# Tile 0's output stores moved behind batch 2's values and into tile 2, a cast's buffer exchanged, and a split load cut elsewhere

## The chip, the cores and the metric

The kernel runs on one core of a Trainium2 chip. Its engines work side by side, each in its own program order: TensorE (PE, with a separate row PEld for weight loads), VectorE (DVE), ScalarE (ACT), GpSimd (POOL) and SyncE (SP). SP only issues transfers here; ACT and POOL issue some as well. The metric is the device time of one execution in microseconds (us). GB/s are those of the profile.

## The reference

Attention in a window of 32 positions to each side, for 8 batches of 8 heads, 576 positions and 64 features, and then a two-layer network with a tanh GELU on the 4608 tokens:

```python
scores = scale * np.matmul(q, k.transpose(0, 1, 3, 2))      # (8, 8, 576, 576)
mask = np.abs(pos[:, None] - pos[None, :]) <= 32
scores = np.where(mask, scores, -1000000000.0)
attn = softmax(scores)
x = np.matmul(attn, v).transpose(0, 2, 1, 3).reshape(4608, 512)
h = x @ w_in                                                # 512 to 2048
out = gelu_tanh(h) @ w_out                                  # 2048 to 512
```

Inputs and output are float32. The kernel computes in float16 with sums in float32.

## The kernel before, in words

**Tiles and batches.** The attention result of all tokens goes as `xT` (features on partitions) into a ring of 1536 tokens. The network runs over nine tiles of 512 tokens, `t` from 0 to 8; a batch has 576 tokens. While tile `t` is in work, the attention of batch `b = t + 1` is done in between. Each turn of the loop over `t` (L810) has two halves. In the first, `ffn_in` multiplies the tile by `w_in` in 16 columns (`fc`), each followed by a GELU on ACT (L540); for `t` from 1 on, DVE makes sums of the GELU's results (L575). In the second, `ffn_out` multiplies by `w_out`: tile 0 in the plain way (`ffn_out_0`), the later tiles with seven products of block sums (`WINO`), 112 steps `i`. The plans `PLAN_0`, `PLAN_1` and `PLAN` say at which step `i` a piece of attention is put between: `s` are the scores of a group of two heads (L427 on PE, the exponential on ACT, L439), `m` the mask on DVE (L445), `v` the sums and the product with V (L450, L460), `x` the result's way into `xT` (L495). PE does all of this in the order of the program, with no engine choosing for it.

**What a batch needs.** In the first half of a tile `cast_and_turn` casts the queries to float16 on DVE (L352), and SP sends them through a transposing transfer to `QT` (L355). `keys()` does the same for the keys (L375, and two transfers to `KT`, L377). The last 64 positions, the tail, go separately: `QT` once more and `KL`. The product with V wants V in two alignments; `pair_v` makes the second by copies on DVE (L192, L193). `load_qk` (L165) has SP load the queries, keys and tails of the batch after; from batch 3 on POOL loads V with a cast in the transfer (L183, L187), behind a small copy (L849) that waits until `KL` has landed.

**Batch 2 is special.** Its keys are cast at `fc == 3` of tile 1 (L822), its tail queries and tail keys on ACT (L361, L367) at `fc` 9 to 13. Its V comes in float32 by SP, in four chunks, issued at L383 behind the key transposes, into the buffer of an earlier query load, and its tail at L371. POOL casts the chunks (`cast_v`, L297, called at L830) and the tail (`cast_vt`, L294, called at step `i == 30` of tile 1, L912). DVE pairs four heads at `i == 17` and four at `i == 40` (L914).

**Tile 0's output.** `ffn_out_0` leaves four blocks of 128 tokens by 512, 256 KB each, in `later`, in the order of the blocks 0, 3, 1, 2 (L611). Entries 0 and 2 share a tile in the place `qt16` of the pool `hp`; entries 1 and 3 are in the pool `yp`. They are stored in tile 1: at `fc == 5` POOL issues 0 and 2 and ACT issues 1, at `fc == 6` ACT issues 3 (L825 to L828). All later tiles are stored by POOL, eight or nine transfers a tile (L594), with the last tile's by SP and ACT. The tail queries of each batch are cast into a tile of that place `qt16` too, and so wait until entries 0 and 2 are out.

**The beginning.** Batch 0's V chunks are loaded by SP at L151 and, the fourth, at L230, in two transfers of 120 and 8 partitions, followed in SP's order by `w_in` (L209). PE fills waits with `spin`, products that nobody reads. The first wait on V in batch 0 is behind POOL's casts (L297) and DVE's pairs (L198, L200); the fourth chunk is cast by DVE (L746) and ACT (L747).

Of the kernel before, what the change touches and what calls it, by code (L numbers as in the profile page):

```python
# [10 lines left out]
FP16 = mybir.dt.float16  # L11
# [25 lines left out]
def cut(b):  # L37
    return 120 if b else 128
# [33 lines left out]
def kernel(  # L72
# [9 lines left out]
    nc = tc.nc  # L82
# [3 lines left out]
    NPAIR = H // 2  # L86
# [15 lines left out]
    rawp = ctx.enter_context(tc.tile_pool(name="rawp", bufs=2))  # L102
    hp = ctx.enter_context(tc.tile_pool(name="hp", bufs=1))
# [85 lines left out]
    def pair_v(b, copy, hs=slice(0, H)):  # L189

        V = Vs[b % 2]
        copy(V[64:128, 4:8, hs, :], V[64:128, 0:4, hs, :])  # L192
        copy(V[0:64, 4:7, hs, :], V[0:64, 1:4, hs, :])  # L193
# [32 lines left out]
    qk(6)  # L226
    load_table(exp_set)
    vs(4, 0, 1, 2)
    for p in (slice(0, 120), slice(120, 128)):
        nc.sync.dma_start(raws[0][3][p, 3, :, :], v[0, :, 384 + p.start:384 + p.stop, :].rearrange("h p d -> p h d"))  # L230
    wi = []
    for i in range(4):
# [49 lines left out]
    def cast_open(b):  # L282
        halfs[b] = [hp.tile([128, NPAIR, 4, 2, 64], FP16, name="q16"),
                    hp.tile([128, NPAIR, 4, 2, 64], FP16, name="k16")]
        QTs[b] = ap_.tile([128, NPAIR, 4, 144], FP16, name="QT")
# [7 lines left out]
    def cast_vt(b):  # L293
        nc.gpsimd.tensor_copy(Vs[b % 2][0:64, 7, :, :], raws[b][4])  # L294

    def cast_v(b, c, copy=nc.gpsimd.tensor_copy):
        copy(Vs[b % 2][:, c, :, :], raws[b][3][:, c, :, :])  # L297
# [6 lines left out]
    def trans_tails(b, pt, half=slice(0, 128), copy=nc.vector.tensor_copy):  # L304
        t16 = halfs[b][2]
        for pr in range(NPAIR):
            nc.tensor.transpose(pt[:, pr, half], t16[half, 2 * pr:2 * pr + 2, :], idn[half, half])
        if half.stop > 64:
            copy(KLs[b % 2], pt[:, 0:4, 64:128])
        if half.start < 64:  # L310
            nc.vector.tensor_copy(QTs[b][:, :, :, 128:144],
                                  pt[:, 0:4, 0:64].rearrange("d r (p j) -> d r j p", j=4))
# [25 lines left out]
    def cast_and_turn(b):  # L338
        cast_open(b)
        q16, k16 = halfs[b]  # L340
        qr, kr, qt, kt = raws[b]
        small = {}

        def tails_of(which):
            if which not in small:
                small[which] = hp.tile([16, NPAIR, 4, 2, 64], FP16, name="qt16", tag="qt16") if which == "q" else \
                    hp.tile([64, NPAIR, 2, 64], FP16, name="kt16", tag="t16")
            return small[which]

        def queries(src, dst, p0, p1):  # L350
            for pr in range(NPAIR):
                nc.vector.tensor_copy(  # L352
                    dst[:, pr, :, :, :].rearrange("p j h d -> p h j d"),
                    src[:, 2 * pr:2 * pr + 2, :].rearrange("p h (j d) -> p h j d", j=4))
            nc.sync.dma_start_transpose(QTs[b].rearrange("d r j p -> d (r j) p")[:, :, p0:p1],  # L355
                                        dst.rearrange("p r j h d -> p (r j h d)"))

        def rest(i):
            qt16, kt16 = tails_of("q"), tails_of("k") if i == 4 else None
            if i < NPAIR:  # L360
                nc.scalar.copy(qt16[:, i, :, :, :].rearrange("p j h d -> p h j d"),  # L361
                               qt[:, 2 * i:2 * i + 2, :].rearrange("p h (j d) -> p h j d", j=4))
            if i == 3:
                nc.sync.dma_start_transpose(QTs[b].rearrange("d r j p -> d (r j) p")[:, :, 128:144],
                                            qt16.rearrange("p r j h d -> p (r j h d)"))
            if i == 4:
                nc.scalar.copy(kt16.rearrange("p r h d -> p (r h d)"), kt.rearrange("p h d -> p (h d)"))  # L367
                nc.sync.dma_start_transpose(
                    KLs[b % 2], kt16.rearrange("p r h d -> p (r h d)"))
                raws[b].append(tailp.tile([64, H, 64], FP32, name="vt", tag="vt"))  # L370
                nc.sync.dma_start(raws[b][4], v[b, :, 512:S, :].rearrange("h p d -> p h d"))  # L371

        def keys():
            for pr in range(NPAIR):
                nc.vector.tensor_copy(k16[:, pr, :, :, :], kr[:, :, 2 * pr:2 * pr + 2, :])  # L375
                if pr % 2:
                    nc.sync.dma_start_transpose(  # L377
                        KTs[b % 2][:, pr - 1:pr + 1, :].rearrange("d r (c p) -> d (r c) p", c=4),
                        k16[:, pr - 1:pr + 1, :, :, :].rearrange("p r c h d -> p (r c h d)"))
            if b == 2:  # L380
                vr = rawp.tile([128, 4, H, 64], FP32, name="qr")
                for c in range(4):
                    nc.sync.dma_start(vr[:, c, :, :],  # L383
                                      v[b, :, 128 * c:128 * c + 128, :].rearrange("h p d -> p h d"))
                raws[b] = [None, None, None, vr]

        queries(qr, q16, 0, 128)
        if b == 2:
            combine(2, nc.vector)
            combine(3, nc.vector)  # L390
            return keys, rest
        keys()
        qt16, kt16 = tails_of("q"), tails_of("k")
        queries(qt, qt16, 128, 144)
        nc.vector.tensor_copy(kt16.rearrange("p r h d -> p (r h d)"), kt.rearrange("p h d -> p (h d)"))
        nc.sync.dma_start_transpose(
            KLs[b % 2], kt16.rearrange("p r h d -> p (r h d)"))
# [140 lines left out]
    def gelu(t, n):  # L538
        fc = column(t, n)
        nc.scalar.activation(gTs[t][:, fc, :], phs[fc], AF.Gelu_apprx_tanh)  # L540
        if t and n % 4 == 3:
            sums(t, n // 4)
# [20 lines left out]
    def combine(i, eng):  # L563
        dst, x, y = wino["todo"][i]
        eng.tensor_tensor(dst, x, y, op=ALU.subtract)
# [14 lines left out]
    def store(t, t4, yo, cols=slice(0, 512), *engs):  # L580

        m = i = 0
        while m < 128:
            b, c = divmod(t * 512 + t4 * 128 + m, S)
            q0, n = (0, cut(b)) if c < 4 * cut(b) else (cut(b), 144 - cut(b))
            j, p = divmod(c - 4 * q0, n)
            e = min(n - p, 128 - m)
            nj = 1 if p else max(1, min(4 - j, (128 - m) // n))
            eng = engs[i % len(engs)] if engs else nc.gpsimd
            if nj > 1:  # L590
                e = nj * n
                eng.dma_start(out_v[b, j:j + nj, q0:q0 + n, cols], yo[m:m + e, cols])
            else:
                eng.dma_start(out_v[b, j, q0 + p:q0 + p + e, cols], yo[m:m + e, cols])  # L594
            m += e
            i += 1

    later = []
# [211 lines left out]
    for t in range(NT):  # L810
        b = t + 1
        att = b < B
        if t:
            for fc in range(begun):
                ffn_in(t, fc, 3, 4, then=False)
            for fc in range(begun):
                gelu(t, fc)
            if att and b > 1:
                parts = cast_and_turn(b)
            for fc in range(begun, NF):  # L820
                ffn_in(t, fc)
                if t == 1 and fc == 3:  # L822
                    parts[0]()
                    combine(4, nc.vector)
                if t == 1 and fc in (5, 6):  # L825
                    for i in (0, 2) if fc == 5 else ():
                        store(0, *later[i])
                    store(0, *later[2 * fc - 9], slice(0, 512), nc.scalar)  # L828
                if t == 1 and 6 <= fc < 10:
                    cast_v(2, fc - 6)  # L830
                if t == 1 and 9 <= fc < 14:
                    parts[1](fc - 9)
                if t == 1 and fc == 8:
                    trans_tails(1, psO.tile([128, 8, 128], FP16, name="pt", tag="O"))
                if t > 1 and fc == 8 and att:
                    pair_v(b, nc.vector.tensor_copy)
        plan = PLAN_0 if not t else PLAN_1 if t == 1 else PLAN if att else {5: "v-1", 31: "x-1"} if t == B - 1 else {}
# [9 lines left out]
        for i in range(113 if t else 65):  # L847
# [62 lines left out]
                    spread(*group(g), *ods[g])  # L910
            if t == 1 and i == 30:
                cast_vt(2)  # L912
            if t == 1 and i in PAIR_1:
                pair_v(2, nc.vector.tensor_copy, PAIR_1[i])  # L914
            if t == 0 and i < 64:
# [39 lines left out]
```

## Time and profile before

| what | us |
|---|---|
| median of 6 runs | 305.05 (304.02 to 305.98) |
| profiled execution, its own time | 305.47 |
| its span | 303.7 |
| PE busy | 291.3 (96%) |
| DVE busy | 194.3 (64%) |
| ACT busy | 194.1 (64%) |
| POOL busy | 90.3 (30%) |
| mean granted PE clock | 0.988 |

The page gives the busy time of each engine, the span in 40 slices with the granted PE clock and the DMA engines' share, the queues, and groups of instructions by line. A line of the timeline gives the start, the duration, the engine, the line of the kernel, what is written from what, and in brackets how long the engine stood idle before it and what ended that. A line of the waits gives who waited for whom, the total, how often, and the longest. Queues are called SPq, ACTq and POOLq; issuing is not counted as busy. The trace also records when each transfer's parts land, by semaphore; these are the landing records that the prediction speaks of.

### The profile page before, as it was taken

The numbers are of one execution on the slowest core, as the hardware profiler recorded it, in microseconds if no ns is written. First come the engines' busy times: TensorE is split into PE (matmuls) and PEld (weight loads), VectorE is DVE, ScalarE is ACT, GpSimd is POOL, SyncE is SP. The second block draws the span as 40 slices with busy tenths as digits, with TensorE's granted clock in tenths as the row PEclk, the third lists the DMA queues.
The fourth block names the chain that finished last, engine by engine and source line by source line (L and its number), as shares of the span: only waits on it lengthen the run. The fifth ranks groups of instructions, "written<-read, shape, count | busy, mean of one in ns | idle before, by whom it ended". The sixth has DMA issues, their size and how long they took to land.

```text
span 303.7 us, 7125 instructions
## 1 busy us (share of the span) xinstructions
PE 291.3 (96%) x2894; PEld 180.7 (59%) x2894; DVE 194.3 (64%) x438; ACT 194.1 (64%) x309; POOL 90.3 (30%) x141
## 2 busy tenths in 40 slices
PE   8789999999799999999999999999999999999994
PEld 3534443446575478647864786478547864784583
DVE  4663548887658866875687668766876634533452
ACT  5855679379566686668666866786578757705600
POOL 3435417300546060603262236050520050016000
PEclk9989999999899999999999999999999999999999
DMA  7999999999699999696999999989597031004013
GB/s 219 234 331 376 309 312 252 256 205 240 169 217 179 170 230 176 124 120 177 196 180 147 208 184 167 154 215 167 84 180 79 3 76 65 2 0 139 2 35 104
DMA packets 116557, 50.73 MB, mean 167 GB/s; under 512 B 97918, under 2 KB 109950, under 8 KB 116525
## 3 DMA queue, kind: packets, MB, share of 16 engines
q1 hardware_dynamic: 87339, 37.88, 62.5%
q0 software_dynamic: 27776, 10.83, 25.2%
q10 hardware_dynamic: 1410, 1.58, 1.7%
q8 instruction: 22, 0.36, 0.6%
q14 instruction: 10, 0.08, 0.1%
HBM read 36.70 MB, written 9.44 MB: 152 GB/s over the span
## 4 chain that ended last, share of the span: by engine, by line
PE 67%; DMA 20%; SPq 8%; DVE 2%; POOL 1%; issue 1%; ACT 0%
PE mm L630 31%; PE mm L532 15%; PE ph L532 12%; DMA wst<-in_moe_w_out_dram 6%; DMA KT<-k 5%; DMA wst<-in_moe_w_in_dram 4%; PE ps_s L427 3%; SPq L175 3%; PE ps_d L450 2%; DMA kr<-in_k_dram 2%; PE ps_o L460 2%; DMA tr<-in_k_dram 2%; SPq L209 2%; DMA qr<-in_v_dram 2%; SPq L151 1%; SPq L383 1%
## 5 line engine op out<-in xcount | busy, mean ns | idle before, releaser
L532 PEld LDWEIGHTS <-w_in 128*128 128x128 f16 x576 | 56.6, 98 | 68.0 <-issue 2.8
L532 PE MATMUL mm<-xT,w_in 128*128 128x512 f16 x304 | 75.7, 382 | 0.3 <-DVE yo L610 0.3
L540 ACT ACTIVATE gT<-mm 128x512 f16<-128x512 f32 x76 | 45.1, 597 | 40.3 <-PE mm L532 39.6
L532 PE MATMUL ph<-xT,w_in 128*128 128x512 f16 x272 | 69.1, 383 | 0.1
L594 POOL DMA_DIRECT2D out_dram<-y x55 | 33.0, 608 | 86.0 <-DVE y L659 77.8
L630 PEld LDWEIGHTS <-s 128*128 128x128 f16 x512 | 49.9, 99 | 6.5
L575 DVE TENSOR_TENSOR s<-gT 128x512 f16<-128x512 f16 x64 | 26.8, 419 | 36.1 <-ACT gT L540 36.1
L540 ACT ACTIVATE gT<-ph 128x512 f16<-128x512 f32 x68 | 37.9, 600 | 15.5 <-PE ph L532 15.5
L630 PE MATMUL mm<-t,s 128*128 128x256 f16 x376 | 46.0, 276 | 0.0
L630 PEld LDWEIGHTS <-gT 128*128 128x128 f16 x384 | 36.0, 98 | 6.9
L439 ACT ACTIVATE pe<-ps_s 128x960 f16<-128x960 f32 (+1 forms) x32 | 30.4, 975 | 10.9 <-PE ps_s L427 10.8
L630 PE MATMUL mm<-w_out,gT 128*128 128x256 f16 x256 | 33.8, 277 | 0.0
L97 ACT ACT_TABLE_LOAD x17 | 21.8, 1283 | 2.2 <-issue 1.9
L486 ACT ACTIVATE lt<-lt 128x480 f32<-128x480 f32 (+3 forms) x36 | 21.1, 585 | 1.1
L485 ACT ACTIVATE lt<-ps_d 128x480 f32<-128x480 f32 (+2 forms) x28 | 15.5, 555 | 9.0 <-PE ps_d L450 6.7
L460 PEld LDWEIGHTS <-V 128*64 128x64 f16 x520 | 14.1, 111 | 9.3 <-DVE V L193 2.4
L445 DVE TENSOR_TENSOR pe<-pe,band 128x960 f16<-128x960 f16 x28 | 18.6, 686 | 1.4 <-ACT pe L439 1.4
L183 POOL DMA_DIRECT2D V<-in_v_dram x20 | 17.9, 911 | 1.3 <-issue 0.7
L630 PE MATMUL mm<-t,gT 128*128 128x256 f16 x128 | 16.5, 273 | 0.0
L427 PE MATMUL ps_s<-QT,KT 64*64 64x128 f16 (+3 forms) x576 | 13.9, 216 | 0.6 <-DMA KT<-k 0.3
L630 PE MATMUL mm<-w_out,s 128*128 128x256 f16 x120 | 14.4, 273 | 0.0
L575 DVE TENSOR_TENSOR s<-s,gT 128x512 f16<-128x512 f16 x32 | 13.6, 425 | 1.1
(110 smaller groups left out, 321.3 us busy)
## 6 DMA issues: line engine op xcount, KB each, us to landing
kr<-in_k_dram SPq DMA_DIRECT2D x31, 256.0 KB, 11.1
qr<-in_q_dram SPq DMA_DIRECT2D x6, 1024.0 KB
wst<-in_moe_w_in_dram SPq DMA_DIRECT2D x8, 512.0 KB, 7.4
wst<-in_moe_w_out_dram SPq DMA_DIRECT2D x3, 1024.0 KB, 11.3
V<-in_v_dram POOLq DMA_DIRECT2D x20, 128.0 KB, 8.6
qr<-in_q_dram SPq DMA_DIRECT2D x7, 256.0 KB
vr<-in_v_dram SPq DMA_DIRECT2D x7, 256.0 KB, 6.2
out_dram<-y POOLq DMA_DIRECT2D x6, 192.0 KB, 6.1
```

Of the source, the lines that this page charges most:

```text
L97: nc.scalar.add_instruction(mybir.InstLoadActFuncSet(name=nc.get_next_instruction_name(), act_func_set_id=which, ins=[], outs=[]))
L183: nc.gpsimd.dma_start(V[:, c, :, :], v[b, :, 128 * c:128 * c + 128, :].rearrange("h p d -> p h d"))
L427: nc.tensor.matmul(ps[64 * half:64 * half + 64, h, 4 * n * r:4 * n * r + 4 * n].rearrange("k (j p) -> k j p", j=4)[:, :, p0 - q0:p1 - q0], ...
L439: nc.scalar.activation(pe, ps[:, :, 0:w], AF.Exp, scale=SCALE)
L445: nc.vector.tensor_tensor(pe, pe, m.rearrange("k (o j) p -> k o j p", o=1).broadcast_to(list(pe.shape)), op=ALU.mult)
L460: nc.tensor.matmul(o[64 * h:64 * h + 64, cols].rearrange("d (j p) -> d j p", j=4)[:, :, p0 - q0:p1 - q0], Vs[b % 2][:, slot, 2 * pr + h, : ...
L486: nc.scalar.activation(lt[:, 0:n], lt[:, 0:n], AF.Exp, scale=-1.0)
L532: nc.tensor.matmul(ph, w_in16[:, dc, fc * 128:fc * 128 + 128], xT[:, dc, t * 512 % RING:t * 512 % RING + 512], start=(dc == 0), stop=(dc = ...
L540: nc.scalar.activation(gTs[t][:, fc, :], phs[fc], AF.Gelu_apprx_tanh)
L575: nc.vector.tensor_tensor(dst, x, y, op=op)
L594: eng.dma_start(out_v[b, j, q0 + p:q0 + p + e, cols], yo[m:m + e, cols])
L630: nc.tensor.matmul(pys["apart"][:, 0:256] if apart else py[:, blk, :], lhsT, wino[w][:, f, :], start=(new and i % (8 if one else 16) == 0) ...
```

## The change

Tile 0's entries 0 and 2 are stored by POOL in tile 1 after step `i == 30`, behind the cast of batch 2's V tail, and entries 1 and 3 by POOL in tile 2 (there they stand, in POOL's order, behind tile 1's output stores and ahead of the copy of L849 and batch 4's V loads). ACT stores nothing of tile 0 any more. Because entries 0 and 2 now stay longer, batch 2's tail queries are cast into a tile of the pool `rawp`, in the place of the key loads (`kr`); those of the later batches use `qt16` as before. The fourth V chunk of batch 0 is loaded as 88 and 40 partitions. No instruction of PE or DVE changes its order.

```diff
-    for p in (slice(0, 120), slice(120, 128)):
+    for p in (slice(0, 88), slice(88, 128)):
         nc.sync.dma_start(raws[0][3][p, 3, :, :], v[0, :, 384 + p.start:384 + p.stop, :].rearrange("h p d -> p h d"))
...
-                small[which] = hp.tile([16, NPAIR, 4, 2, 64], FP16, name="qt16", tag="qt16") if which == "q" else \
+                small[which] = rawp.tile([16, NPAIR, 4, 2, 64], FP16, name="qt16", tag="kr") if which == "q" and b == 2 else \
+                    hp.tile([16, NPAIR, 4, 2, 64], FP16, name="qt16", tag="qt16") if which == "q" else \
                     hp.tile([64, NPAIR, 2, 64], FP16, name="kt16", tag="t16")
...
-                if t == 1 and fc in (5, 6):
-                    for i in (0, 2) if fc == 5 else ():
-                        store(0, *later[i])
-                    store(0, *later[2 * fc - 9], slice(0, 512), nc.scalar)
...
+                if t == 2 and fc in (8, 9):
+                    store(0, *later[1 if fc == 8 else 3])
...
             if t == 1 and i == 30:
                 cast_vt(2)
+                store(0, *later[0])
+                store(0, *later[2])
```

## The prediction

> **What bounds the kernel now.** I read TensorE's waits first, then its timeline around the longest, then the clock there, and last the queues that feed it. The waits (engine, line, tile; us in total, times, longest):
>
> ```profile
> PE ps_od L460 <- DVE V L193: 2.1, 1, 2.1
> PE mm L460 <- DVE V L200: 1.3, 2, 1.0
> ...
> PE mm L460 <- POOL V L297: 1.1, 1, 1.1
> ...
> PE ps_s L427 <- DMA KT<-k: 0.3, 1, 0.3
> ```
>
> PE is busy 291.3 us of the 303.7 us span, so time can come only from its few stalls. Two of the three large ones lie before 18 us; the largest is in tile 1, in PE's timeline (start, us):
>
> ```profile
> 78.04 0.21 PE L460 MATMUL ps_od<-pe,V 128*64 128x96 f16 x2
> 80.37 0.38 PE L460 MATMUL ps_od<-pe,V 128*64 128x64 f16 x12 [2.13 <-DVE V L193]
> ```
>
> The stretches after it (clock is the column before DMA's share and GB/s):
>
> ```profile
> 80.00:84.00 4.00, 3.63 (x43) 2.73 (x44) 3.89 (x9) 2.71 (x5) 2.32 (x4) 0.67 0.89 250
> 84.00:88.00 4.00, 4.00 (x70) 2.68 (x70) 1.60 (x3) 2.68 (x4) 2.08 (x3) 0.91 1.63 234
> ```
>
> So the stall is paid twice: 2.13 us idle, and 4 x 0.33 + 4 x 0.09 = 1.68 us of clock lost behind it, 3.81 us together. What made V late, on DVE, ACT, SP and POOL:
>
> ```profile
> 65.75 1.43 DVE k L375 x4
> ...
> 63.43 0.38 ACTq L594 DMA_DIRECT2D out_dram<-yo  x1
> ...
> 66.94 4.27 SPq L377 DMA_TRANSPOSE KT<-k  x2
> 71.26 4.25 SPq L383 DMA_DIRECT2D qr<-in_v_dram  x4
> ...
> 78.82 0.61 POOL L297 CAST V<-qr 128x512 f16<-128x512 f32 x1 [0.17 <-DMA qr<-in_v_dram]
> 81.68 0.71 POOL L294 CAST V<-vt 64x512 f16<-64x512 f32 x1 [2.25 <-DMA vt<-in_v_dram]
> ...
> 108.39 0.35 POOL L849 COPY after<-KL 128x1 f16<-128x1 f16 x1 [10.39 <-DMA KL<-kt]
> ```
>
> Batch 2's keys land at 65.73, DVE casts them after 1.00 us of waiting, SP issues transposes and V loads in order, POOL casts the last chunk at 78.82, DVE pairs it (0.42 + 0.42), PE goes on at 80.37.
>
> **The stores leave 58 to 70 us.** Four stores of 256 KB: two from POOL (issued 58.25 and 59.98), two from ACT (63.43, 64.30). ACT loses two issues of 0.37 us, each inside idle time before a GELU that waits for PE: nothing. The bytes matter. POOL's pair, 0.52 MB, moves before the keys land; at the 273 GB/s of 56 to 64 that is 1.9 us, of which only the 1.00 us that DVE waits counts. ACT's pair moves beside the transposes; at 235 GB/s (68 to 72) it is 2.2 us. V thus comes 1.0 (if the transposes are bound by SP's issue) to 4.1 us earlier; I take 1.0 + 2.2 = 3.2, since the landing records show the query transpose landing at 71.69, right behind the last ACT store (71.48). PE needs V 2.13 us earlier. The stall goes, with a us to spare.
>
> Here a rule and a row differ. The Trainium skill, "TensorE: Matmul & The Clock Gate", section "Why this matters for your kernels", warns of gaps over about 3 us: one window of idle drops the clock by half. The trace has the half clock behind a gap of only 2.13 us. By the rule the stall would be worth 2.13 us, by the row 3.81. I use the row for this execution, but the same page (section "What's actually happening") calls the window free-running, so a given gap may or may not be punished; nothing in one trace shows how often.
>
> **Stores 0 and 2, now behind POOL's cast of V's tail.** Two issues of 0.75 us = 1.5 us on POOL. Queued behind them: the small copy of L849 and batch 3's V loads (82.52 now). The tail also lands some 2.9 us earlier (the 3.2 less what SP's issue keeps), so these loads start about 1.3 us earlier than now, and their first user (DVE's pair at 102.92) is far away: nothing. The bytes, 0.52 MB at 250 GB/s, take 2.1 us, of which loads in another queue lose less: by the records some 1.3 us where POOL's pair moved earlier. SP reaches batch 3's loads (79.33 now) 2.9 us earlier. Net on batch 3's keys and tails: -2.9 + 2.1 = -0.8 us, cautiously.
>
> **Stores 1 and 3, in tile 2.** POOL does not wait for PE there: they follow tile 1's last output store (ends 98.0) at once, 1.5 us of issue. L849 and the V loads behind them are covered by 10.39 us of POOL idle, and no buffer of theirs is wanted again. Their bytes fall on batch 3's transposes (SP issues queries at 96.01, keys 101.05 to 104.5). The landing records give the first keys at 106.38; PE reads them at 107.96. That slack of 1.6 us is all the cover. PE will come 3.81 us earlier, at 104.15; so this is the next thing late. Keys land at 106.38 - 0.8 + x. Bounds of x: 0 or a little less, if the stores fill holes (the DMA share is 0.78 in 96 to 100); 0.52 MB at 155 GB/s = 3.4 us if they displace the transposes at the rate of 96 to 100. Rows near: from the issue of the queries to the first keys, tiles 2 to 6 take 10.4, 12.2, 10.8, 10.0 and 12.0 us. In tiles 4 and 6 POOL's stores go on 4.2 us past that issue, in the others 2.1: 11.4 against 10.9. The change makes tile 2 like tiles 4 and 6, though with more bytes: x = 0.5. So PE starts the scores at 106.1 instead of 107.96: of the 3.81 us, 1.9 are kept and 1.9 become a wait for KT.
>
> **The tail queries' buffer.** Four ACT casts of 0.60 us go to a buffer of the key pool; same instructions, no wait that ends late (its former content, batch 1's keys, was last read by 43.6). Batch 3's keys go to the buffer that batch 2's casts left by 67.2. Batch 3's tail queries use the old buffer, which stores 0 and 2 hold: sent by 81.5, they land in 4 to 5 us, before the cast at 97.48. All three: nothing.
>
> **88 and 40 partitions.** Two SP issues stay two (1.25 and 1.01 us). The records show 15 engines' landings for the 120 rows, from 15.57 to 17.26, and 8 for the 8 rows. The skill's "DMA: Bandwidth & Descriptors" ("Why a DMA increments its semaphore by 16 and not by 1") says the largest divisor up to 16 is used: 15 and 8, as seen, and now 11 and 10, the lowest-numbered. That speaks against the edit: by the rule the ten busiest engines carry 64 + 32 pieces instead of 64 + 8. By the row the last to land was one straggler at 17.26 that had few pieces more than the others (16.29), and if it is among the engines left out, the chunk lands earlier. Neither end reaches PE: ACT's cast waits 0.44 us for this chunk, but DVE's (17.66) stands behind chunk 2's pair (17.14 to 17.73), with 0.4 us to spare. Bounds -0.3 to +0.4; I take 0.
>
> **Sum.** The profiled execution took 305.47 us (303.7 of span, 1.8 around it), 0.4 above the median of 305.05. 305.47 - 3.81 + 1.9 = 303.6. I state this, without a further 0.4: executions with less time may lack one half-clock stretch, and then gain less.
>
> **The rivals.**
> (a) *The gain becomes a KT wait and a half clock in tile 2.* PE idles 1.9 us there, nearly the 2.13 that was punished in tile 1. If it is, 1.7 us come back: 305.3. Or x = 2.2 without the clock: 303.6 + 1.7 = 305.3 as well. For it: the size, and that the half clock of 20 to 23 us follows waits of only 1.05 and 0.31 us. Against it: the 0.97 us wait before 14.57 and the 0.3 us of tile 3 were not punished.
> (b) *Slower.* Tile 2's transposes lose as much time as the stores' bytes need: x = 2.4 or more, keys at 108.0, later than PE reads them today, after almost 4 us of idle, followed by the half clock: 305.47 + 0.0 + 1.7 = 307.2. For it: in five tiles the queries land within 0.6 us of the last output store, so more stores may simply hold them back; and the skill's section "Issuing engines are not separate DMA queues" says moving a store between ACT and POOL frees no bandwidth, only its place in time. Against it: tiles 4 and 6. With the half clock it decides from keys at 106.3 + 0.9 = 107.2, x = 1.6.
> (c) *The change doesn't do what it says*: V is late for SP's own issue time, and comes only 1.0 us earlier. Then the stall is 1.1 us, without or with the half clock: 302.8 to 304.5, or more with (a); a small case.
>
> **How the numbers follow.** A measurement here tells about 0.3% (0.9 us) from no change. Forecast 0.43 (its own range 302.3 to 304.5), (a) 0.26, (b) 0.26, (c) 0.05. Faster takes the forecast but for its upper end, and the better part of (c): 0.44; same takes most of (a) and what is left: 0.25; slower takes (b) and the upper end of (a): 0.31. Low end: the forecast with x = 0 and the keys 0.8 us sooner still, 303.6 - 1.3 = 302.3. High end: most of (b), 306.8, just below its 307.2.
>
> **What would show it.** V's last cast on POOL near 75.6 instead of 78.82 and no wait of L460 for L193; clock 1.00 from 80 to 88; a wait of L427 for KT or QT near 104 to 106 of about 1.9 us, and the clock behind it; ACT without stores; L297's first wait in batch 0 unchanged. If V's cast moves less than 2 us, the first step is wrong; if the KT wait exceeds 3 us, x is; if PE's early waits move by over 0.5 us, the split matters after all.

## The result, and the profile after

The changed kernel takes 301.68 us (median of 35 runs, 299.91 to 304.28), against 304.92 for the one before (72 runs): a ratio of 0.9907 with a 95% interval of 0.989 to 0.9925. It is faster by 0.9%, and the time lies below the range that was forecast (302.3 to 306.8). The profiled execution took 301.78, its span is 300.0, 3.7 less than before. (The ratios here leave disturbed runs out, and so can differ from the quotient of the two medians.)

PE's waits after the change, as before (engine, line, tile; us in total, times, longest). The lines of the kernel that are shown here have moved down by one:

```profile
PE mm L605 <- DVE w_out L218: 1.4, 2, 1.1
PE mm L461 <- DVE V L200: 1.4, 2, 1.1
...
PE mm L461 <- POOL V L297: 0.9, 1, 0.9
PE ps_s L428 <- DMA KT<-k: 0.6, 2, 0.3
...
PE ps_od L461 <- DVE V L193: 0.2, 1, 0.2
```

The line that led the list, the wait for V's pair, has gone from 2.1 to 0.2 us. The forecast's new wait, 1.9 us for KT in tile 2, is not there: of the 0.6 us for KT, 0.27 lie in tile 2, and 0.31 in tile 3, where it was 0.28 before. PE's timeline, around the old stall and at the start of tile 2 and of its scores:

```profile
77.73 0.21 PE L461 MATMUL ps_od<-pe,V 128*64 128x96 f16 x2
78.17 0.38 PE L461 MATMUL ps_od<-pe,V 128*64 128x64 f16 x12 [0.23 <-DVE V L193]
...
89.80 0.81 PE L533 MATMUL mm<-xT,w_in 128*128 128x512 f16 x3
...
104.47 0.62 PE L428 MATMUL ps_s<-QT,KT 64*64 64x96 f16 x32 [0.27 <-DMA KT<-k]
```

Before, PE stood at 78.25 when it ran out of V, went on at 80.37, and began tile 2 and its scores here:

```profile
93.62 0.81 PE L532 MATMUL mm<-xT,w_in 128*128 128x512 f16 x3
...
107.96 0.62 PE L427 MATMUL ps_s<-QT,KT 64*64 64x96 f16 x32
```

So PE is now 0.3 us ahead at the stall, 2.2 behind it, 3.8 at tile 2, and still 3.5 at the scores. The step from 2.2 to 3.8 is the clock, 1.00 now in both stretches behind the stall (the column before DMA's share and GB/s):

```profile
80.00:84.00 4.00, 4.00 (x73) 2.91 (x71) 2.90 (x8) 3.76 (x7) 3.55 (x5) 1.00 1.18 287
84.00:88.00 4.00, 4.00 (x66) 3.05 (x66) 2.25 (x5) 2.91 (x6) 0.69 (x1) 1.00 1.81 190
```

What brings V, on SP and POOL:

```profile
61.63 3.52 SPq L356 DMA_TRANSPOSE QT<-q  x1
65.25 2.63 SPq L378 DMA_TRANSPOSE KT<-k  x2
67.93 3.12 SPq L384 DMA_DIRECT2D qr<-in_v_dram  x4
...
75.55 0.61 POOL L297 CAST V<-qr 128x512 f16<-128x512 f32 x1 [1.04 <-DMA qr<-in_v_dram]
```

POOL casts V's last chunk at 75.55 instead of 78.82; the key transposes are issued in 2.63 us instead of 4.27 and V's chunks in 3.12 instead of 4.25. That chain came as forecast (75.6). What did not come is tile 2's loss.

### The profile page after: what moved, and what is told of

Read it like the earlier page. It is cut to its first block, busy times and chain, and to the rows that moved or that the text cites. A ratio compares the mean times of both kernels' runs of the same rounds, so it can differ in the third digit from the quotient of the medians.

```text
span 300.0 us, 7127 instructions
## 1 busy us (share of the span) xinstructions
PE 287.8 (96%) x2894; PEld 179.2 (60%) x2894; DVE 193.9 (65%) x438; ACT 194.0 (65%) x309; POOL 92.6 (31%) x143
## 4 chain that ended last, share of the span: by engine, by line
PE 70%; DMA 16%; SPq 7%; DVE 3%; ACT 2%; issue 1%; POOL 1%
PE mm L631 31%; PE mm L533 16%; PE ph L533 14%; DMA wst<-in_moe_w_out_dram 5%; DMA KT<-k 5%; DMA wst<-in_moe_w_in_dram 4%; PE ps_s L428 3%; PE ps_d L451 2%; SPq L151 2%; PE ps_o L461 2%; SPq L209 1%; DMA kr<-in_k_dram 1%; SPq L230 1%; ACT gT L541 1%; SPq L213 1%; SPq L149 1%
## 5 line engine op out<-in xcount | busy, mean ns | idle before, releaser
L533 PE MATMUL mm<-xT,w_in 128*128 128x512 f16 x304 | 74.8, 379 | 0.1
L533 PE MATMUL ph<-xT,w_in 128*128 128x512 f16 x272 | 68.2, 379 | 0.1
L576 DVE TENSOR_TENSOR s<-gT 128x512 f16<-128x512 f16 x64 | 27.6, 431 | 36.6 <-ACT gT L541 36.6
L541 ACT ACTIVATE gT<-ph 128x512 f16<-128x512 f32 x68 | 37.9, 600 | 13.3 <-PE ph L533 13.3
L631 PE MATMUL mm<-t,s 128*128 128x256 f16 x376 | 45.0, 273 | 0.0
L848 POOL COPY after<-KL 128x1 f16<-128x1 f16 x5 | 1.6, 315 | 45.5 <-DMA KL<-kt 45.5
```

The source lines that it names most:

```text
L533: nc.tensor.matmul(ph, w_in16[:, dc, fc * 128:fc * 128 + 128], xT[:, dc, t * 512 % RING:t * 512 % RING + 512], start=(dc == 0), stop=(dc = ...
L576: nc.vector.tensor_tensor(dst, x, y, op=op)
L631: nc.tensor.matmul(pys["apart"][:, 0:256] if apart else py[:, blk, :], lhsT, wino[w][:, f, :], start=(new and i % (8 if one else 16) == 0) ...
```

## The experiments

Each is told with its edit, what was expected of it, and what came. "Before" was run beside each group on the same chip; its medians there are 305.1, 305.0, 305.3 and 306.5 us. In the diffs `OLD` stands for the four lines at L825 to L828.

### One part of the change at a time

**Only the 88/40 split.**

```diff
-    for p in (slice(0, 120), slice(120, 128)):
+    for p in (slice(0, 88), slice(88, 128)):
```

> Only the split of batch 0's fourth V chunk is changed (88 and 40 rows for 120 and 8); the stores stay. Theory (the gain is batch 2's V coming earlier): nothing, 304.9 within 0.5, the wait of PE for V's pair in tile 1 stays at 2.1 us. Rival (the gain is made at the beginning: the changed kernel's trace has no half clock near 20 us, the one before has): 303.2, and no half clock at 20 us.

305.20 us, ratio 0.9982 [0.9954, 1.0009]; the wait for V's pair is 2.8 us, with the half clock behind it. The split alone does nothing that can be told. Nor was the gain made at the beginning, the rival: the granted clock of this trace has the same lower digit near 20 us as before, and so has that of the change without the split, which gains in full.

**Only POOL's pair (entries 0 and 2) moved**, with the tail queries' other buffer; ACT stores 1 and 3 as before.

```diff
                 if t == 1 and fc in (5, 6):
-                    for i in (0, 2) if fc == 5 else ():
-                        store(0, *later[i])
                     store(0, *later[2 * fc - 9], slice(0, 512), nc.scalar)
...
                 cast_vt(2)
+                store(0, *later[0])
+                store(0, *later[2])
```

> Only stores 0 and 2 (POOL's pair) are moved behind the V casts, with the tail queries' buffer; ACT still stores 1 and 3. Theory: batch 2's keys land 1.4 us earlier, DVE casts them 1.0 us earlier, V follows by about 1.0 us, the wait shrinks from 2.1 to about 1.1 us; with some of the half clock gone too 303.2 to 304.0. Rival (only the bytes beside the transposes matter): V moves less than 0.3 us, 304.9.

302.92 us, 0.9965 [0.9935, 0.9994]. The keys' cast begins at 64.31 instead of 65.75 and waits 0.3 us instead of 1.0; V's pair is waited for 0.86 us, and the clock stays at 1.00.

**Only ACT's pair (1 and 3) moved** into tile 2.

```diff
-OLD
+                if t == 1 and fc == 5:
+                    for i in (0, 2):
+                        store(0, *later[i])
...
+                if t == 2 and fc in (8, 9):
+                    store(0, *later[1 if fc == 8 else 3])
```

> Only stores 1 and 3 (ACT's pair) are moved, to POOL in tile 2; POOL still stores 0 and 2 early. Theory: V's last cast about 2.2 us earlier (76.6), the wait is nearly gone, 302.0 to 302.6; a wait for KT in tile 2 of 0 to 0.5 us. Rival (SP's own issue sets V's time): V moves less than 1 us, 304 or more.

302.93 us, 0.9932 [0.9909, 0.9955]. The keys' cast stands where it stood (65.86), but the query transpose takes 6.3 us to land instead of 9.3; the wait for V's pair is 0.42 us.

**The change without the split** (120 and 8 as before).

```diff
-    for p in (slice(0, 88), slice(88, 128)):
+    for p in (slice(0, 120), slice(120, 128)):
```

> The changed kernel with the split undone (120 and 8 rows). Theory: as the changed kernel, 301.7 within 0.5. Rival (beginning): 303.3, with the half clock back at 20 us.

301.80 us (6 runs), 0.9890 [0.9849, 0.9931], wait 0.21: the changed kernel's time without its split. By the ratios POOL's pair alone gains 0.35%, ACT's 0.68%, both together 0.93%. In the traces either pair alone leaves a stall under 1 us and no half clock behind it, so there the parts overlap; the intervals of the times are too wide to say by how much.

### What the half clock is worth

**Before, with the stall filled** by ten products that nobody reads, ahead of tile 1's first product with V. It adds work of PE and changes nothing that is computed.

```diff
+        if fill:
+            for _ in range(fill):
+                nc.tensor.matmul(o, w_in16[:, 0, 0:128], w_in16[:, 0, 0:512], start=True, stop=True)
         times(b, g, o, pe)
```

> The kernel before, with ten more products of 128x512 on PE, put where it stalls in tile 1 (behind the sums of batch 2's first group, ahead of the product with V); nobody reads them, so the output is as before. They fill 10 x 0.215 = 2.15 us of the 2.13 us wait. Theory (the half clock behind the stall is a second cost): the profile shows no half clock near 81 us, PE's tile 2 begins up to 1.7 us earlier; over many executions, of which only some had it, a gain of 0.3 to 1.0 us: 304.1 to 304.8. Rival (the half clock has nothing to do with the idle time, or costs nothing): 305.1, or 305.3 if the filling overruns the wait.

305.05 us, 1.0002 [0.9971, 1.0033]. Its traced execution was a lone one of 1030 us and says nothing. The same kernel once more:

> The kernel before with ten products that nobody reads in the stall before tile 1's first product with V, once more, for a profile. If the half clock behind the stall is worth its 1.7 us, the clock is 1.00 from 80 to 88 us and PE reaches tile 2's scores 1.5 us earlier than before, 303.3 to 304.0. If filling costs as much as it gives (the ten products take longer than the stall), the clock is 1.00 and tile 2's scores begin where they did, 304.7 to 305.3.

304.55 us, 1.0001 [0.9976, 1.0026]. In this trace the clock is 1.00 from 80 to 88 us, and PE needs 11.7 us from the stall's end to tile 2 instead of 13.25. But the fill kept PE until 79.81, while DVE's pair of V was ready at 79.07 (78.65 + 0.42), so 0.7 us of it were pure work. By the trace that leaves half of what the clock gave; the times show none of it. Nor does this trace show that filling keeps the clock whole: without the fill PE would have stood here for only 1.5 us (77.61 to 79.07), and stalls of up to 1.69 us at this place had no half clock behind them in the other runs. No version with a shorter fill was run, so the price of the half clock stays a reading of traces.

### Bytes, or their place

**All four stores on POOL, early in tile 1**, nothing else changed.

```diff
-                    store(0, *later[2 * fc - 9], slice(0, 512), nc.scalar)
+                    store(0, *later[2 * fc - 9])
```

> The kernel before with all four stores issued by POOL at their early place; only the issuing engine of stores 1 and 3 differs. They then leave about 2 us earlier (right behind store 2, near 61 us). Theory (bytes in that stretch are what costs): as before, 305.1 within 0.7, wait of 1.5 to 2.5 us. Rival (ACT's queue beside the transposes is what costs): the wait falls below 1.2 us, 303.5.

302.32 us, 0.9925 [0.9902, 0.9948], where I had expected 305.1. All 1.05 MB still leave ahead of V; only that POOL has issued the last of them by 60.84, where ACT issued at 63.43 and 64.30. The wait is 1.07 us. So a price per byte does not describe these stores.

**Entries 1 and 3 in tile 3 instead of tile 2.**

```diff
-                if t == 2 and fc in (8, 9):
+                if t == 3 and fc in (8, 9):
```

> The changed kernel with stores 1 and 3 in tile 3 instead of tile 2. Theory (their bytes lengthen the way from the queries' transpose to the first keys, 12.3 us in the changed kernel's tile 2 against 10.4 before): 10.4 to 11 us in tile 2, no wait for KT there, about 1.8 us more in tile 3, where the wait for KT was 0.3 us and becomes about 2 us, perhaps with a half clock: 303 to 304.5. Rival (their bytes cost nothing in either tile): 301.7 within 0.5.

302.95 us, 0.9924 [0.9894, 0.9954]. The wait for KT that was expected in tile 3 did not come; the trace has none. But it is not better than the change: taking these stores out of tile 2 brings nothing that can be told.

**Entries 1 and 3 stored twice in tile 2**, 0.52 MB more, the same values.

```diff
                     store(0, *later[1 if fc == 8 else 3])
+                    store(0, *later[1 if fc == 8 else 3])
```

> The changed kernel with stores 1 and 3 each sent twice in tile 2 (the same bytes to the same place), 0.52 MB more. Theory (each 0.52 MB there puts off the first keys by about 1.9 us; the cover is used up): from the queries' issue to the first keys 14 us, wait for KT in tile 2 2.0 to 2.4 us, often with a half clock: 303.5 to 305. Rival (the transposes don't lose by stores; the 12.3 us are chance): wait of 0.3 to 0.6 us, 301.8.

301.98 us, 0.9912 [0.9878, 0.9946]. The edit missed its aim. POOL issued the second copy of an entry only when the first had landed (the first at 101.78):

```profile
97.28 0.58 POOL L595 DMA_DIRECT2D out_dram<-yo  x1
102.34 1.09 POOL L595 DMA_DIRECT2D out_dram<-yo  x2 [4.48 <-DMA out_dram<-yo]
```

The fourth followed at 108.96. Batch 3's first keys landed at 102.49, so only one of the four stores lay in their way, and PE did not wait for KT in tile 2; the 1.2 us for KT in this trace lie in tile 3. What twice the bytes beside tile 2's transposes would cost was not measured.

### Queue, or moment

After the run with all stores on POOL two theories stood: the *moment* counts (stores in flight beside the query transpose hold it back), or the *queue* does (ACT's stores are dearer than POOL's).

**ACT's stores some columns earlier.**

```diff
-OLD
+                if t == 1 and fc == begun:
+                    for i in (0, 2):
+                        store(0, *later[i])
+                if t == 1 and fc in (begun, begun + 1):
+                    store(0, *later[1 if fc == begun else 3], slice(0, 512), nc.scalar)
```

> The kernel before, with ACT's two stores (entries 1 and 3) issued by ACT still, but some 3 us earlier, at the first two columns of tile 1 (near 60.5 us). Theory 1, the moment counts (stores that flow beside the query and key transposes hold them back): ACT's stores are out before the transposes, the query transpose lands near 68.2, the wait for V's pair falls to about 1.1 us, 302.3 to 302.8, like the run with all four stores on POOL. Theory 2, the queue counts (ACT's stores are slow to start or disturb whatever their moment): the wait stays at 1.8 us or more, 304.5 to 305.3.

303.37 us, 0.9974 [0.9939, 1.0009]: undecided, and the edit missed its aim. ACT had three GELUs ahead of them, and issued the stores at 62.32 and 63.19, only 1.1 us earlier than before. They were still in flight beside the transpose. (The trace is of the slowest of its 14 executions, 306.46.)

**ACT's stores ahead of its first GELU.**

```diff
+            if t == 1:
+                for i in (1, 3):
+                    store(0, *later[i], slice(0, 512), nc.scalar)
             for fc in range(begun):
                 gelu(t, fc)
```

(and `OLD` stores 0 and 2 only)

> The kernel before, with ACT's two stores issued by ACT ahead of tile 1's first GELU (near 59 us), as early as POOL had them in the run with four stores on POOL. If the moment counts, whatever the queue: the stores land by 66, V's wait falls to 1.1 us or less without a half clock behind it, 302.3 to 302.9. If ACT's queue is what costs: the wait stays at 2 us, 304.5 to 305.3. If the two issues delay the GELUs so that PE waits for PSUM, PE shows a wait for ACT near 60 to 62 us, and up to 0.7 us of the gain is lost.

303.30 us beside 306.49 for before, 0.9918 [0.9884, 0.9952]: the gain of the run with all on POOL, from ACT's queue. ACT's issues and PE's stall in its trace:

```profile
58.14 0.37 ACTq L594 DMA_DIRECT2D out_dram<-yo  x1
58.70 0.36 ACTq L594 DMA_DIRECT2D out_dram<-yo  x1
...
79.25 0.38 PE L460 MATMUL ps_od<-pe,V 128*64 128x64 f16 x12 [0.86 <-DVE V L193]
```

**Entries 1 and 3 on POOL at ACT's moment**: each behind a copy of 128x1 that waits for a GELU.

```diff
-                    store(0, *later[2 * fc - 9], slice(0, 512), nc.scalar)
+                    nc.gpsimd.tensor_copy(after, gTs[t][:, column(t, fc - 1), 0:1])
+                    store(0, *later[2 * fc - 9])
```

> The kernel before, with entries 1 and 3 issued by POOL instead of ACT at the same moment as before: each behind a copy of 128x1 that waits for a GELU of tile 1 (near 63.4 and 64.3 us). Theory 1, the moment counts: nothing is gained, the wait for V's pair stays near 2 us, 304.5 to 305.3. Theory 2, the queue counts: the wait falls to about 1 us, 302.3 to 302.8.

302.68 us, 0.9923 [0.9896, 0.9950]. By the time alone the queue would have won. Its traced execution, though, was one of 304.07. Again, for a second trace:

> The run with entries 1 and 3 stored by POOL at ACT's moment, unchanged, for a second trace, because its first traced execution was slower than its median by 1.4 us. If POOL's stores hold the query transpose back as ACT's do, it lands right behind the last store again, near 71 to 72 us, and V's wait is 1 us or more. If POOL's queue is the gentler one, the transpose lands at 70 or earlier and V's wait is under 0.8 us.

302.62 us (one run). POOL's two late issues, and PE's stall:

```profile
62.05 0.55 POOL L594 DMA_DIRECT2D out_dram<-yo  x1
...
63.23 0.54 POOL L594 DMA_DIRECT2D out_dram<-yo  x1 [0.28 <-issue]
...
78.59 0.38 PE L460 MATMUL ps_od<-pe,V 128*64 128x64 f16 x12 [1.69 <-DVE V L193]
```

The landing records decide it. For each trace: when the query transpose of batch 2 was issued, when the last store then under way landed, when the transpose landed, and how long it took (us):

```
                                 issued  last store   landed   took
before                            62.40     71.48      71.69    9.3
before, second trace              62.20     71.23      71.43    9.2
split only                        63.08     72.82      73.03   10.0
stall filled                      62.17     70.45      70.68    8.5
only 0 and 2 moved                61.19     69.25      69.45    8.3
ACT 1.1 us earlier                62.00     72.62      72.84   10.8
POOL at ACT's moment              63.30     71.69      71.89    8.6
POOL at ACT's moment, second      61.32     70.04      70.07    8.8
all four on POOL, early           61.80     65.70      68.14    6.3
ACT ahead of the GELUs            63.91     66.33      69.54    5.6
only 1 and 3 moved                62.47     65.03      68.73    6.3
changed kernel                    61.63      none      67.23    5.6
changed kernel, second trace      62.55      none      68.06    5.5
```

In all eight traces in which stores are under way up to its landing, the transpose lands within 0.25 us behind the last of them, 8.3 to 10.8 us after its issue, whichever engine issued them. Where they are through early or come later it needs 5.5 to 6.3 (4.9 to 7.0 with the four traces that the table leaves out). The same is seen in tile 2: in eleven of the twelve traces without stores of tile 0 there, batch 3's query transpose lands within 0.3 us behind the last output store of tile 1. The queue is refuted as a cause of the late landing; the moment stands. That agrees with the Trainium skill, "DMA: Bandwidth & Descriptors", section "Issuing engines are not separate DMA queues", by which the transfers of all issuing engines run interleaved on the same DMA engines.

The times do not follow the landing, and that stays open: with POOL at ACT's moment little but the issuing engine differs from before, and yet its 302.7 us are as good as the early stores'. Its two traces keep more than half of the stall (1.16 and 1.69 us) but have no half clock at all. The clock is a part of its gain: over its 13 executions the granted clock averages 0.9946, against 0.9921 in the 45 of before beside it, which is some 0.8 us of 303 by an estimate from these two, where the ratio is worth 2.3. Where the rest comes from is not shown.

**Another mixture**: 1 and 3 by POOL early, 0 and 2 behind V's tail cast, so that tile 2 holds none.

```diff
-                if t == 2 and fc in (8, 9):
-                    store(0, *later[1 if fc == 8 else 3])
+                if t == 1 and fc == 5:
+                    for i in (1, 3):
+                        store(0, *later[i])
```

> The changed kernel, with entries 1 and 3 stored by POOL early in tile 1 (where the run with four stores on POOL had them) and entries 0 and 2 behind V's tail cast as in the change; so nothing of tile 0 is stored in tile 2. If tile 2's stores cost the changed kernel its KT waits (0.6 us), this is the best version: wait for V's pair under 0.5 us, none for KT, 300.9 to 301.4. If what is left there is unrelated, 301.5 to 302.0, as the changed kernel. If the early pair holds the keys back, the wait for V is 0.5 to 1.0 and the time 302.0 to 302.5.

302.44 us, 0.9922 [0.9895, 0.9950]: wait for V's pair 0.73 us, and 0.58 for KT although tile 2 has no stores of tile 0. There POOL issued tile 1's own last output store 5.3 us after batch 3's query transpose, where it is 1.3 before. No version was faster than the changed kernel by more than the intervals can tell.

### How typical the traces are

**Before, unchanged, once more.**

> The kernel before, unchanged, for a second trace: is the stall before V's pair as long in every execution, and is it always followed by the half clock? If the stall is the program's, it is 2.0 to 2.8 us again and V's last cast stands 13 us behind the first key cast; then an execution without the half clock still has the stall and takes about 304.0. If the first trace was an unlucky one, the stall is under 1.5 us.

306.60 us. The stall is 1.97 us, with V's last cast at 78.57, and the product behind it runs at a lower clock: 0.53 us for what takes 0.38 at full clock (128x64), 0.61 for 0.40.

```profile
80.13 0.53 PE L460 MATMUL ps_od<-pe,V 128*64 128x64 f16 x12 [1.97 <-DVE V L193]
80.85 0.61 PE L460 MATMUL ps_o<-pe,V 128*64 128x96 f16 x14
```

**The change, unchanged, once more.**

> The changed kernel, unchanged, for a second trace: how much of tile 2's time from the issue of batch 3's query transpose to its first keys (12.25 us in the first trace, 10.0 in runs with twice or none of tile 2's stores) belongs to the stores? If it is the stores, it is 11.5 or more again, with a wait for KT of 0.2 us or more; if it varies by itself, about 10 and no wait for KT.

302.66 us, no half clock anywhere, no wait for V's pair, 0.47 us for KT. From the issue of batch 3's query transpose to its first keys it takes 12.45 us, after 12.25 in the first trace. That speaks for the stores, the more so as the 10.0 of the run with twice the stores was a way with only one of them in it; against it stand the 12.56 us of the other mixture, without any of them, though there tile 1's own stores ran late.

## Why the prediction was wrong

**The stall's cause and size: right.** V was to come 3.2 us earlier, with the last cast at 75.6; it came 3.27 earlier, at 75.55. The stall was to go: 0.23 us are left. The half clock was to go: PE's way from the stall's end to tile 2 fell from 13.25 to 11.63 us, 1.62 where I had 1.68. PE began tile 2 3.82 us earlier where I had 3.81. The reason I gave for it, bytes times a rate, was right only by its sum: ACT's pair did not cost its 2.2 us of bandwidth but held the query transpose until it had landed; the same bytes from the same engine 5 us earlier left a stall of 0.86 us.

**The failed step: "Net on batch 3's keys and tails", -0.8 us, and with it the keys at 106.38 - 0.8 + x.** I let the first keys of batch 3 move with their loads. They move with PE. The query transpose is issued behind DVE's cast of the queries, and that cast ends an unbroken run of DVE's work that began with a wait for PE. Before, on DVE and SP:

```profile
92.08 0.69 DVE L659 TENSOR_TENSOR y<-mm,y 128x512 f32<-128x512 f32 x1 [1.65 <-PE mm L630]
...
93.82 0.76 DVE L668 TENSOR_TENSOR y<-mm,y 128x256 f32<-128x256 f32 x2
94.49 1.44 DVE L352 CAST q<-qr 128x512 f16<-128x512 f32 x4
...
96.01 4.95 SPq L355 DMA_TRANSPOSE QT<-q  x1
```

After:

```profile
88.25 0.69 DVE L660 TENSOR_TENSOR y<-mm,y 128x512 f32<-128x512 f32 x1 [1.65 <-PE mm L631]
...
90.00 0.76 DVE L669 TENSOR_TENSOR y<-mm,y 128x256 f32<-128x256 f32 x2
90.67 1.44 DVE L353 CAST q<-qr 128x512 f16<-128x512 f32 x4
...
92.18 4.82 SPq L356 DMA_TRANSPOSE QT<-q  x1
97.09 5.33 SPq L378 DMA_TRANSPOSE KT<-k  x2
```

The cast starts at once behind L668 (L669 after) in both, with no wait for a load. The transpose's issue is 2.39 us behind PE's start of tile 2 before (96.01 - 93.62) and 2.38 after (92.18 - 89.80); it is 2.38 or 2.39 in all seventeen traces (the one of 1030 us left out), though PE starts tile 2 anywhere from 89.80 to 94.81 in them. So the 1.6 us of slack that KT had moved along with PE, and 3.8 us of earlier PE could not use it up; only x could. The lines that show this stood in the trace of before; I read when the loads landed and not what the cast waited for.

**x was too small as well, but that is not what failed.** From the query transpose's issue to the first keys, twelve traces without stores of tile 0 in tile 2 take 9.1 to 12.6 us (mean 10.3), four with both of them in the way 11.3 to 12.5 (mean 12.0), and the one with a single store 10.0. So x is about 1.7 by the means, with a wide spread, and 1.9 in the profiled execution, where I took 0.5. With the right start alone, and x still 0.5, the keys would stand at 106.38 - 3.83 + 0.5 = 103.05, before PE is ready at 104.2, and the sum would be 305.47 - 3.81 = 301.7, against 301.78 measured. With x = 1.9 they stand at 104.45 (measured 104.43), PE waits 0.3, and it is 302.0. Since the failed step lay under the forecast, rival (a), rival (b) and the low end alike, no case held the time.

**The loads themselves** moved further than forecast: SP came to batch 3's loads 3.77 us earlier (2.9 forecast), and the tail keys landed 3.08 us earlier (0.8 forecast). The 2.1 us for stores 0 and 2 beside them was about right as a mean, though only 0.7 appears in these two traces: from SP's first issue to the tail keys' landing it is 17.0 to 18.3 us in ten traces without these stores there (mean 17.7), and 18.7 to 21.3 in seven with them (mean 19.6). No wait of PE came of it.

**Nothing for ACT's issues, for the tail queries' buffer and for the split: right.** No wait on either appears, and the run with the split alone and the one without it show none. The first wait for POOL's cast in batch 0 is 0.9 us after 1.1, and 0.6 and 1.1 in the runs with the split alone and without it. The chunk's last part landed at 17.81 instead of 17.26, 0.55 later where my bound was 0.4. One row of the first trace belongs to it, which I had not listed: 0.3 us of PE waiting for DVE's part of the split chunk; the second trace of the change lacks it.

**The median.** The profiled executions differ by 3.7 us, the medians by 3.2. The prediction left 0.4 for executions that lack a half-clock stretch; the runs bear the direction out. The granted clock averages 0.992 in the three groups of 45 to 55 runs of before (0.990 in the fourth, of 19), and 0.995 in 36 of the change. That is, by an estimate from their four digits (0.9923 over the three groups, 0.9946), about 0.7 us of clock in the mean execution, where the profiled one showed 1.6.

**The rivals.** (a) and (b) fell with KT's wait in tile 2: 0.27 us in the profiled execution, at most 0.47 in the five traces with stores of tile 0 there. (c) fell: V came 3.3 us earlier, not 1.0.

## What to carry to other kernels

Before you give back part of a gain to the next thing that is late, ask what releases that thing: if its start follows the engine that gets faster, its slack travels along, and only what is added to its own way can use it up. Price a store by what is in flight when it flows, not by its bytes: here 0.52 MB beside a transposing transfer cost about 3 us of its landing, and nearly none of it 5 us earlier.

## What the hardware showed that was not expected

- A transposing transfer landed right behind the stores that were in flight with it, within 0.25 us in eight traces of eight, at 8.3 to 10.8 us from its issue instead of 4.9 to 7.0 in the other nine. Whether loads in flight do the same was not tried.
- The half clock came with stalls at this place of 1.97, 2.13, 2.66 and 2.79 us, and with none of the eleven from 0.20 to 1.69 us. So the gap that was punished at this place lay below the 3 us that the Trainium skill warns of ("TensorE: Matmul & The Clock Gate", section "Why this matters for your kernels"); here the traces decide. Length alone is not the rule either: near 20 us, in the trace of before, a half clock stands behind waits of only 1.05 and 0.31 us. Its price, from the stall's end to tile 2, was 1.0 to 1.7 us: 13.0 to 13.3 us against 11.6 to 12.0.
- The profile's row of the granted clock shows a lower stretch near 20 us in some executions and not in others, for kernels whose beginning is the same. Before:

```profile
PEclk9989999999899999999999999999999999999999
```

The changed kernel, first trace:

```profile
PEclk9999999999999999999999999999999999999998
```

The third digit of the first, near 20 us, does not go with the change: both traces of before have it lowered, and so has the change without the split, while the run with all four stores on POOL, whose beginning is that of before, has not. The eleventh, behind the stall, is what the change took away.
